# A transformer layer on one core: the first Strassen product ahead of the output projection, attention's QK one tile at a time, the softmax exp at the end of MLP2

## The chip, the core and the metric

The kernel runs on one core of a Trainium2 chip. The metric is the device time of one execution in microseconds (us), smaller is better. A timed run gives a time, the span of the core and the mean granted clock of TensorE over that span (1.0 is full speed). One execution is also taken by the hardware profiler; its page and its trace are quoted here. A run that is over 1.5% above the fastest of its kernel is counted as slow. Medians and ranges below are of all runs, ratios of the fast ones alone.

The engines in the profile are PE (TensorE's matmuls), PEld (its weight loads), DVE (VectorE), ACT (ScalarE), POOL (GpSimd) and SP (the queue that issues most DMAs). The kernel is scheduled by hand: each engine has its own list of instructions, so the order of two independent instructions on one engine is a decision. A hole is a stretch in which TensorE waits. The halo of a tile is the part of K or V that comes from earlier rows; a DMA fetches it. The gelu tail is what ScalarE still has to do of MLP1's gelus when TensorE has ended MLP1, about 2.8 us.

## The reference

A pre-norm layer on x of 2048 rows and 576 columns, bf16, one batch:

```python
def _A_ref(x, wqkv, wo):                 # H = 32 heads of 18, window W = 8, dilation 2
    qkv = ...(x @ wqkv)...
    idx = pos[:, None] - off[None, :]    # keys at distance 0, 2, .., 14
    logits = jnp.einsum("bhsd,bhswd->bhsw", q, kg) * scale
    attn = _softmax(jnp.where(mask, logits, -1e9))
    return einsum("bhsw,bhswd->bhsd", attn, vg)... @ wo
def _B_ref(x, w1, b1, w2, b2):           # F = 4608
    h = _gelu(_layernorm(x) @ w1 + b1)
    return h @ w2 + b2
h  = x + _A_ref(_layernorm(x), ...)
h2 = h + _B_ref(_layernorm(h), ...)
```

## The kernel before

The 16 token tiles of 128 rows go through the second half of the kernel in eight groups of two. While group k is in its MLP, the attention of group k+2 runs on VectorE (QK, softmax, PV), and group k+1 gets its output projection ("wo") and its second layer norm (LN2). So one turn of the loop contains, on TensorE: MLP1 of group k, the projection of k+1, MLP2 of k.

From group 2 on, MLP2 uses Strassen's scheme on a part of the hidden dimension: seven products instead of eight, on sums of blocks that VectorE prepares (`w2_sums`, `h_sums`); `rows` says how large that part is (8 of 18 pairs of blocks in groups 2 and 3, 12 in 4 and 5, all 18 in 6 and 7), the rest is done plainly. The products accumulate in PSUM banks a, b, d, f and e. Three times ScalarE copies a bank to another one, to be its starting value; this is called a seed here: b from a after product 1, d from b after product 6, f from d after product 5.

```python
def mlp2_fast(g, rows, tags, last, inserts):        # before; cut
    product(1, a, rows, True)
    seed(b, a)                       # ScalarE copy, PSUM to PSUM
    call(inserts.get(1, ()))         # ln2_stats(c, d), h_sums, w2_sums
    product(2, a, rows)              # has to wait until the seed has read bank a
    plain(0, 0, a, rows)
    call(inserts.get(2, ()))         # att_den(e, f)
    product(6, b, rows)
    seed(d, b)
    call(inserts.get(6, ()))         # ln2_send(c), ln2_send(d)
    product(7, e, rows, True)
    add(rest, e..., x_of(j1))
    call(inserts.get(7, ()))         # PV of tile e, ln2_ins
    product(5, d, rows)
    seed(f, d)
    product(4, b, rows); plain(1, 0, b, rows); plain(1, 1, d, rows)
    add(o1, bd, rest); store(j1, o1)
    call(inserts.get(4, ()))         # PV of tile f
    product(3, f, rows); plain(0, 1, f, rows)
    out0(...)
# the loop of one group, k >= 2; cut
    m1[1] = [c_(att_qk_pair, e, f)]  # QK of both tiles of group k+2, during MLP1
    mlp1(g, mlp1_plan(p, q, r, s, True), m1, mid)
    if e is not None:
        exps(e, f)                   # table load, exp, gelu's table load, on ScalarE
    if c is not None:
        wo_visit((c, q), (d, r))     # output projection of group k+1
    mlp2_fast(g, rows, (s, p, q), c is None, x)
```

LN2's statistics are on ScalarE too (`ln2_act`: two passes with accumulators, then a reciprocal root by a power instruction on GpSimd), and so is its application (`ln2_send`), which then goes out to DRAM and comes back through a transposing DMA (`ln2_in`) as the input of the next MLP1.

## Time and profile before

| | before |
|---|---|
| timed runs | 393.6 us median of 4 (392.1 to 394.3) |
| profiled run | 389.87 us, span 388.1 us, mean granted clock 0.995 |
| TensorE, VectorE, ScalarE busy | 361.8, 298.3, 229.8 us |
| TensorE waiting in MLP2 for ScalarE's seeds | 17.2 us in 12 waits |

The page of the kernel before, its first part (busy time, share, instructions) and the head of the fourth (the chain of waits that ended last):

```profile
PE 361.8 (93%) x4904; PEld 297.3 (77%) x4904; DVE 298.3 (77%) x412; ACT 229.8 (59%) x513; POOL 35.1 (9%) x47
...
PE 51%; DVE 32%; ACT 7%; issue 4%; DMA 2%; SPq 1%; POOL 1%; DVEq 0%; ACTq 0%; POOLq 0%
```

Up to about 152 us VectorE leads (LN1, the first tiles' attention). From there on it is TensorE and its holes. The view by windows, one line for each group 2 to 7 (start and end in us, length, then busy time and number of instructions of PE, PEld, DVE, ACT, POOL, then the granted clock, the DMA share and GB/s):

```profile
146.20:190.50 44.30, 38.96 (x498) 33.08 (x498) 35.76 (x40) 23.78 (x57) 2.89 (x4) 0.96 0.32 78
190.50:231.90 41.40, 37.10 (x499) 30.66 (x499) 31.72 (x37) 23.78 (x57) 2.88 (x4) 1.00 0.39 77
231.90:271.80 39.90, 36.62 (x495) 30.28 (x496) 35.21 (x40) 23.87 (x57) 1.95 (x4) 1.00 0.29 67
271.80:311.70 39.90, 36.62 (x495) 30.28 (x496) 33.02 (x37) 23.98 (x57) 2.65 (x5) 1.00 0.33 76
311.70:348.50 36.80, 35.80 (x489) 29.61 (x488) 18.42 (x31) 20.55 (x53) 2.61 (x4) 1.00 0.27 49
348.50:388.00 39.50, 33.77 (x451) 27.98 (x450) 8.90 (x13) 14.73 (x39) 0.00 (x0) 0.99 0.04 13
```

The first two numbers after the window are to be compared: group 2 lasts 44.30 us with 38.96 us of TensorE, group 4 lasts 39.90 us with 36.62 us. Where the difference is, TensorE's timeline shows. Each line has start, length, line, operation, operands and count, and in brackets how long the engine was idle before it and what ended that. Product 1 of group 2, the matmuls after the hole, and product 4:

```profile
167.44 1.16 PE L619 MATMUL po<-w2a_sb,h_all 128*128 128x288 bf16 x8
171.89 4.28 PE L619 MATMUL po<-w2a_sb,h_all 128*128 128x288 bf16 x20 [3.29 <-ACT po L650]
...
181.10 0.65 PE L619 MATMUL po<-x_all,h_all 128*128 128x288 f16 x4 [1.00 <-ACT po L650]
```

TensorE stands still for 3.29 us until the seed is copied. The 20 matmuls after it take 4.28 us; the same 20 in group 3 take 2.61 us. The window of that stretch shows why:

```profile
172.00:177.00 5.00, 5.00 (x29) 3.43 (x28) 2.98 (x5) 3.54 (x10) 1.11 (x2) 0.66 0.01 3
```

The granted clock is 0.66 over these 5 us. In group 3, after a hole of 3.30 us, it stays at 1.00.

What the seed waited for is in ScalarE's timeline, here of group 4, from the last gelus of MLP1 (which ends on TensorE at 249.7 us) to the seed:

```profile
248.04 4.49 ACT L528 ACTIVATE h_all<-pm,b_sb 128x256 f16<-128x256 f32 x12 [1.99 <-PE pm L214]
252.55 1.28 ACT L366 ACT_TABLE_LOAD   x1
253.84 0.63 ACT L366 ACTIVATE logits<-logits 128x512 f32<-128x512 f32 x1
254.49 1.28 ACT L504 ACT_TABLE_LOAD   x1
255.79 0.20 ACT L504 ACTIVATE warm<-mhalf 128x1 f32<-128x1 f32 x1
255.90 0.39 ACT L650 COPY po<-po 128x288 f32<-128x288 f32 x1
```

The gelus end at 252.5, then come a table load, the exp, the load of gelu's table and a dummy instruction that forces it, 3.4 us together, and only then the seed (L650).

### The profile page before, as it was taken

The page shows a single profiled execution, that of the slowest core. Times are in us where ns is not written, and L with a number is a line of the kernel's source. Part 1 is how long each engine was busy: PE and PEld are TensorE (multiplying, and loading weights), DVE is VectorE, ACT ScalarE, POOL GpSimd, SP SyncE. Part 2 cuts the span into 40 slices and gives each one's busy share as a digit, 9 for nine tenths or more (in the row PEclk, how much of TensorE's full clock was granted, in tenths as well). Part 3 has the DMA queues.
Part 4 walks back from the last instruction along what each step waited for, and adds up shares of the span by engine and source line. Part 5 has one row for each costly group of instructions (what it writes and reads, how often), then busy time and mean ns, then how long its engine had stood idle before and what let it go on. Part 6 is the DMA issues. An engine that isn't in the chain of part 4 may idle for free.

```text
span 388.1 us, 11433 instructions
## 1 busy us (share of the span) xinstructions
PE 361.8 (93%) x4904; PEld 297.3 (77%) x4904; DVE 298.3 (77%) x412; ACT 229.8 (59%) x513; POOL 35.1 (9%) x47
## 2 busy tenths in 40 slices
PE   7999999999999998968998799979997999999895
PEld 4789877896788777946886578857885788778774
DVE  6899999999998999895779579978977794420331
ACT  2687747887657833793087806781579247726710
POOL 3240021000220110000100110010101010100000
PEclk9999999999999999989999999999999999999999
DMA  8987798946296355201921074004710350040000
GB/s 244 309 247 221 167 236 265 350 67 188 68 196 183 138 101 112 64 30 51 157 70 47 20 153 106 17 30 111 149 19 31 94 107 17 3 84 17 2 9 24
DMA packets 61875, 43.70 MB, mean 113 GB/s; under 512 B 31856, under 2 KB 60144, under 8 KB 61824
## 3 DMA queue, kind: packets, MB, share of 16 engines
q1 hardware_dynamic: 59936, 41.13, 39.6%
q0 software_dynamic: 1728, 1.77, 4.4%
q8 instruction: 38, 0.62, 0.7%
q10 hardware_dynamic: 160, 0.07, 0.1%
q14 instruction: 13, 0.11, 0.1%
HBM read 21.10 MB, written 12.42 MB: 86 GB/s over the span
## 4 chain that ended last, share of the span: by engine, by line
PE 51%; DVE 32%; ACT 7%; issue 4%; DMA 2%; SPq 1%; POOL 1%; DVEq 0%; ACTq 0%; POOLq 0%
PE pm L214 25%; PE po L619 24%; DVE prod L381 5%; DVE prod L332 5%; DVE prod L326 5%; DVE prod L385 4%; ACT h_all L528 3%; DVE ln_stats L150 2%; PE pw L214 2%; DVE h L439 1%; DMA x_all<-in_A_x_dram 1%; ACT po L650 1%; ACT L504 1%; DVE peak L344 1%; PE pq L214 1%
## 5 line engine op out<-in xcount | busy, mean ns | idle before, releaser
L528 ACT ACTIVATE h_all<-pm,b_sb 128x256 f16<-128x256 f32 (+1 forms) x288 | 108.5, 498 | 94.4 <-PE pm L214 94.4
L214 PE MATMUL pm<-hnT,w_sb 64*128 64x256 bf16 x2304 | 143.1, 269 | 1.5 <-DVE o_sb L692 1.0
L214 PEld LDWEIGHTS <-w_sb 64*128 64x128 bf16 x2304 | 113.7, 94 | 15.1 <-issue 3.5
L619 PEld LDWEIGHTS <-h_all 128*128 128x128 f16 x560 | 55.1, 99 | 36.3 <-issue 22.2
L619 PE MATMUL po<-w2a_sb,h_all 128*128 128x288 bf16 (+1 forms) x332 | 47.3, 293 | 14.7 <-ACT po L650 13.3
L214 PE MATMUL pq<-wq_sb,xnT 64*128 64x288 bf16 x768 | 54.1, 283 | 0.3 <-ACT kv_ring L299 0.2
L214 PEld LDWEIGHTS <-xnT 64*128 64x128 bf16 x864 | 44.0, 94 | 9.1 <-issue 0.4
L332 DVE TENSOR_TENSOR prod<-prod 128x2304 bf16<-128x2304 bf16 (+1 forms) x64 | 44.2, 691 | 2.1
L326 DVE TENSOR_TENSOR prod<-kv_ring,q_all 128x4608 bf16<-128x4608 bf16 x16 | 40.8, 2549 | 6.4 <-DMA kv_ring<-kv_dram 6.3
L381 DVE TENSOR_TENSOR prod<-kv_ring,probs 128x4608 bf16<-128x4608 bf16 x16 | 40.8, 2552 | 0.2
L214 PE MATMUL pm<-hnT,w1h_sb 64*128 64x256 bf16 x288 | 39.5, 269 | 0.0
L385 DVE TENSOR_TENSOR prod<-prod 128x2304 bf16<-128x2304 bf16 (+1 forms) x32 | 33.8, 1058 | 1.1
L542 PEld LDWEIGHTS <-h_all 128*128 128x128 bf16 x288 | 28.0, 98 | 7.7 <-issue 0.7
L542 PE MATMUL po<-w2a_sb,h_all 128*128 128x288 bf16 x224 | 28.3, 286 | 0.0
L455 POOL TENSOR_TENSOR ln_rstd<-ln_var,mhalf 128x1 f32<-128x1 f32 x14 | 10.3, 733 | 198.2 <-ACT ln_var L454 196.8
L619 PEld LDWEIGHTS <-kv_ring 128*128 128x128 f16 x228 | 22.3, 98 | 5.6
L299 ACT CAST kv_ring<-pq 128x576 bf16<-128x576 f32 x32 | 19.4, 641 | 8.4 <-PE pq L214 8.2
L647 DVE TENSOR_TENSOR kv_ring<-po,x_all 128x576 f32<-128x576 f32 x6 | 4.5, 758 | 24.1 <-PE po L619 24.1
L599 DVE TENSOR_TENSOR kv_ring<-h_all 128x1536 f16<-128x1536 f16 (+2 forms) x8 | 6.3, 786 | 21.4 <-ACT h_all L528 21.4
L619 PE MATMUL po<-w2b_sb,h_all 128*128 128x288 bf16 (+1 forms) x152 | 22.2, 286 | 0.0
L214 PE MATMUL pw<-wo_sb,oT 64*128 64x288 bf16 x256 | 19.5, 283 | 0.2
L650 ACT COPY po<-po 128x288 f32<-128x288 f32 x18 | 6.9, 386 | 19.8 <-PE po L619 19.8
(97 smaller groups left out, 386.7 us busy)
## 6 DMA issues: line engine op xcount, KB each, us to landing
w_sb<-in_B_w_dram SPq DMA_DIRECT2D x6, 768.0 KB, 6.3
kv_ring<-kv_dram SPq DMA_DIRECT2D x28, 144.0 KB, 2.9
w2a_sb<-in_B_w_dram SPq DMA_DIRECT2D x4, 1008.0 KB, 6.4
kv_dram<-kv_ring SPq DMA_DIRECT2D x13, 288.0 KB, 4.7
out_dram<-o_sb SPq DMA_DIRECT2D x15, 144.0 KB, 2.0
td<-q_all SPq DMA_DIRECT2D x14, 144.0 KB, 2.2
td<-hn SPq DMA_DIRECT2D x14, 144.0 KB, 1.8
x_all<-in_A_x_dram SPq DMA_DIRECT2D x12, 144.0 KB, 2.3
```

The costliest lines, as they stand in the source:

```text
L150: nc.vector.bn_stats(out=stats[:, i, c, :], in_=src[:, c * HALF:(c + 1) * HALF])
L214: last = nc.tensor.matmul(duo["g"][r ^ swap][i], lhsT=lhsT, rhs=rhs, start=(swap == 0 and i == 0 and kt == 0), stop=(swap == 1 and kt == K ...
L299: pace[0] = nc.scalar.copy(out=dst.rearrange("p (d g h) -> p g d h", g=2, h=H // 2), in_=ps[:, :, 0:HALF].rearrange("p g (h d) -> p g d h" ...
L326: nc.vector.tensor_tensor(out=prod[:], in0=k_ring[j % 2], in1=q_all[:, j, :].unsqueeze(1) .to_broadcast([P, W, D]), op=ALU.mult)
L332: nc.vector.tensor_tensor(out=prod[:, :, o * H:o * H + n], in0=prod[:, :, a * H:a * H + n], in1=prod[:, :, c * H:c * H + n], op=ALU.add)
L381: nc.vector.tensor_tensor(out=prod[:].rearrange("p w (d h) -> p w d h", h=H), in0=v_ring[j % 2].rearrange("p w (d h) -> p w d h", h=H), in ...
L385: nc.vector.tensor_tensor(out=prod[:, 0:n, :], in0=prod[:, 0:n, :], in1=prod[:, n:2 * n, :], op=ALU.add)
L455: nc.gpsimd.tensor_tensor(out=rstd[:], in0=var[:], in1=mhalf[:], op=ALU.pow)
L528: pace[0] = nc.scalar.activation(out=hT(grp)[:, f, 0:N], in_=ps[:, r, i * N:(i + 1) * N], func=ACT.Gelu_apprx_tanh, bias=b1_sb[:, f:f + 1] ...
L542: nc.tensor.matmul(banks[half], lhsT=hT(grp)[:, f, i * P:(i + 1) * P], rhs=w2_rows(f)[:, half * HALF:(half + 1) * HALF], start=(f == 0), s ...
L619: nc.tensor.matmul(bank, lhsT=l, rhs=r, start=start, stop=stop, skip_group_check=True)
L650: nc.scalar.copy(out=to, in_=bank)
```

## The change

The intent is to fill the hole from both sides: product 1 goes ahead of the projection, so that its seed runs while TensorE does the projection, and exp with its two table loads goes behind the last seed of MLP2. Attention had to be taken apart for this, since normalization and PV follow exp: QK of tile e is now computed a turn earlier, in MLP2, and QK of tile f in MLP1, with the logits of alternate groups in two places; PV of tile e is at the end of MLP2 and PV of f at the start of the next MLP1. Half of `h_sums` moves into MLP1. The seeds get new places between the steps of LN2. The core of the diff, cut:

```diff
-        product(1, a, rows, True)
-        seed(b, a)
...
+        if rows <= SR:        # groups 2 to 5
+            steps = [(1, all_), "b", "wo", "h", "e", (2, all_), "11", (6, all_), "6", "d", "7", (7, all_), "rest", "in",
+                     (5, all_), "f", "exp", (4, all_), "21", "22", "o1", "4", (3, all_), "12", "o0", "3"]
+        elif not last:        # group 6
+            steps = [(1, lo), "wo", "h", "e", (1, hi), "b", (7, lo), (6, all_), "6", "d", "7", (2, all_), (7, hi), "rest", "in",
+                     (5, all_), "f", (4, all_), "o1", (3, all_), "o0"]
+        else:                 # group 7
+            steps = ["e", (1, lo), (7, lo), (1, hi), "b", "h", (7, hi), "rest", (6, all_), "d", (2, all_), "lo",
+                     (5, all_), "f", (4, all_), "o1", (3, all_), "o0"]
...
-                m1[1] = [c_(att_qk_pair, e, f)]
+                m1[0] += [c_(pv_sum, d), c_(send_o, d), c_(read_o, d)]
+                m1[1] = [c_(att_qk_one, f, 1, home ^ 1), c_(att_max, (e, f))]
+                m1[3] += [c_(h_sums, 0, rows, (0, 2))]
+                x["h"] += [c_(h_sums, 0, rows, (1, 3))]
+                x["exp"] += [c_(exps, e, f), c_(att_den, e, f)]
+                x["4"] += [c_(att_pv_a, e), c_(halo, e, 2)]
+                x["3"] += [c_(att_pv_b, e), c_(send_o, e), c_(read_o, e)]
...
+                x["7"] += [c_(att_qk_one, GROUPS[k + 3][0], 0, home)]
...
+                x["h"] = [c_(ln2_stats, c, d)] + x["h"]
+                x["6"] += [c_(ln2_send, c)]
+                x["7"] = [c_(ln2_send, d)] + x["7"]
+                x["in"] = [c_(ln2_ins, c, d)] + x["in"]
```

In `steps` a tuple is a product with its rows, a letter b, d or f is a seed, "wo" the projection, "11" to "22" the plain part, "o1" and "o0" the output sums; the others are hooks for the lists of `x`.

More of the change, by code (lines that the diff above doesn't have):

```diff
@@ L314, with logit_of @@
     side = {}
+    def logit_of(js):
+        home, i = side[js[0]]
+        return (x_all[:, 13:16:2, 0:2 * W * H].bitcast(F32).rearrange("p i (w h) -> p i w h", w=W)
+                if home else logits[:])[:, i:i + len(js)]
     def sides(js):
-        i = side[js[0]]
+        i = side[js[0]][1]
         return slice(i, i + len(js))
@@ L333, in att_qk_add, with att_qk_b @@
                                     in1=prod[:, :, c * H:c * H + n], op=ALU.add)
-    def att_qk_b(j, i, skip=0):
-        side[j] = i
+    def att_qk_b(j, i, skip=0, home=0):
+        side[j] = (home, i)
+        out = logit_of([j])[:, 0]
         att_qk_add(j, ((0, 0, 9), (0, 0, 4), (0, 0, 2), (0, 0, 1))[skip:])
-        nc.vector.tensor_tensor(out=logits[:, i], in0=prod[:, :, 0:H], in1=prod[:, :, 8 * H:9 * H], op=ALU.add)
+        nc.vector.tensor_tensor(out=out, in0=prod[:, :, 0:H], in1=prod[:, :, 8 * H:9 * H], op=ALU.add)
         if j // 2 + 1 < W:
-            nc.vector.memset(logits[0:1, i, j // 2 + 1:W, :], -1e9)
+            nc.vector.memset(out[0:1, j // 2 + 1:W, :], -1e9)
     def att_max(js):
-        n, sl = len(js), sides(js)
-        nc.vector.tensor_reduce(out=peak[:, sl], in_=logits[:, sl].rearrange("p i w h -> p i h w"), axis=AX.X, op=ALU.max)
-        nc.vector.tensor_tensor(out=logits[:, sl], in0=logits[:, sl],
-                                in1=peak[:, sl].unsqueeze(2).to_broadcast([P, n, W, H]), op=ALU.subtract)
+        n, sl, lg = len(js), sides(js), logit_of(js)
+        nc.vector.tensor_reduce(out=peak[:, sl], in_=lg.rearrange("p i w h -> p i h w"), axis=AX.X, op=ALU.max)
+        nc.vector.tensor_tensor(out=lg, in0=lg, in1=peak[:, sl].unsqueeze(2).to_broadcast([P, n, W, H]), op=ALU.subtract)
     def att_qk_rest(j, i, skip=0):
@@ L355, in att_qk, with att_qk_one @@
         att_qk_rest(j, i)
-    def att_qk_pair(e, f):
-        for i, j in enumerate((e, f)):
-            att_qk_a(j)
-            halo(j, 1)
-            att_qk_b(j, i)
-        att_max([e, f])
+    def att_qk_one(j, i, home):
+        att_qk_a(j)
+        halo(j, 1)
+        att_qk_b(j, i, 0, home)
     def att_exp(*js):
-        sl = sides(js)
-        nc.scalar.activation(out=logits[:, sl], in_=logits[:, sl], func=ACT.Exp, scale=SCALE)
+        lg = logit_of(js)
+        nc.scalar.activation(out=lg, in_=lg, func=ACT.Exp, scale=SCALE)
     def att_pv(j):
@@ L372, in att_den, with att_pv_a @@
     def att_den(*js):
-        n, sl = len(js), sides(js)
-        nc.vector.tensor_reduce(out=den[:, sl], in_=logits[:, sl].rearrange("p i w h -> p i h w"), axis=AX.X, op=ALU.add)
+        n, sl, lg = len(js), sides(js), logit_of(js)
+        nc.vector.tensor_reduce(out=den[:, sl], in_=lg.rearrange("p i w h -> p i h w"), axis=AX.X, op=ALU.add)
         nc.vector.reciprocal(out=den[:, sl], in_=den[:, sl])
-        nc.vector.tensor_tensor(out=probs[:, sl], in0=logits[:, sl],
-                                in1=den[:, sl].unsqueeze(2).to_broadcast([P, n, W, H]), op=ALU.mult)
-    def att_pv_sum(j):
-        a = probs[:, side.pop(j)]
+        nc.vector.tensor_tensor(out=probs[:, sl], in0=lg, in1=den[:, sl].unsqueeze(2).to_broadcast([P, n, W, H]), op=ALU.mult)
+    def att_pv_a(j):
+        a = probs[:, side.pop(j)[1]]
         nc.vector.tensor_tensor(out=prod[:].rearrange("p w (d h) -> p w d h", h=H),
@@ L383, in att_pv_sum, with att_pv_b @@
                                 in1=a.unsqueeze(2).to_broadcast([P, W, Dh, H]), op=ALU.mult)
+    def att_pv_b(j):
         for n in (4, 2):
@@ L386, in att_pv_sum @@
         nc.vector.tensor_tensor(out=q_all[:, j, :], in0=prod[:, 0, :], in1=prod[:, 1, :], op=ALU.add)
+    def att_pv_sum(j):
+        att_pv_a(j)
+        att_pv_b(j)
     oT, hn, hnT, h_of = {}, {}, {}, {}
@@ L619, in mm, with product @@
         nc.tensor.matmul(bank, lhsT=l, rhs=r, start=start, stop=stop, skip_group_check=True)
-    def product(n, bank, rows, start=False):
+    def product(n, bank, m0, m1):
         lhs, rhs = PRODUCTS[n]
-        for m in range(rows):
-            mm(bank, lhs(m), rhs(m), start and m == 0, m == rows - 1)
+        for m in range(m0, m1):
+            mm(bank, lhs(m), rhs(m), n in (1, 7) and m == 0, m == m1 - 1)
     def plain(i, half, bank, rows):
@@ L635, in halves, with mlp2_fast @@
         return ap.rearrange("p (g c) -> p g c", g=2)
-    def mlp2_fast(g, rows, tags, last, inserts):
+    def mlp2_fast(g, rows, tags, wo, hooks):
+        p, q, r, s = tags
+        last = wo is None
         j0, j1 = g
-        af, bd, ee = (psum_pair(tag, "po") for tag in tags)
+        af, bd = (psum_pair(tag, "po") for tag in (q, p))
         a, f, b, d = (pair[:, n, 0:HALF] for pair in (af, bd) for n in range(2))
-        e = ee[:, 0, 0:HALF]
         o0, o1 = (late.tile([P, D], BF16, tag="o_sb", name="o_sb", bufs=2) for _ in range(2))
@@ L644, in mlp2_fast @@
         rest = halves(flat[:, W * 2 * D - 2 * D:W * 2 * D].bitcast(F32))
+        bank = {1: a, 2: a, 3: f, 4: b, 5: d, 6: b}
         def add(out, x, y):
             nc.vector.tensor_tensor(out=out, in0=x, in1=y, op=ALU.add)
-        def seed(to, bank):
-            nc.scalar.copy(out=to, in_=bank)
-        def store(j, o, n=slice(0, 2)):
-            cols = slice(n.start * HALF, n.stop * HALF)
-            nc.sync.dma_start(out=out3[:, j, cols], in_=o[:, cols])
-        def out0(n=slice(0, 2)):
-            add(halves(o0[:])[:, n], af[:, n, 0:HALF], halves(x_of(j0))[:, n])
-            store(j0, o0, n)
@@ L660, in mlp2_fast @@
-        product(1, a, rows, True)
-        seed(b, a)
-        call(inserts.get(1, ()))
-        product(2, a, rows)
-        plain(0, 0, a, rows)
-        if last:
-            out0(slice(0, 1))
-        call(inserts.get(2, ()))
-        product(6, b, rows)
-        seed(d, b)
-        call(inserts.get(6, ()))
-        product(7, e, rows, True)
-        add(rest, e.unsqueeze(1).to_broadcast([P, 2, HALF]), halves(x_of(j1)))
-        call(inserts.get(7, ()))
-        product(5, d, rows)
-        seed(f, d)
@@ L676, in mlp2_fast, with out0 @@
-        call(inserts.get(5, ()))
-        product(4, b, rows)
-        plain(1, 0, b, rows)
-        plain(1, 1, d, rows)
-        add(halves(o1[:]), bd[:, :, 0:HALF], rest)
-        store(j1, o1)
-        call(inserts.get(4, ()))
-        product(3, f, rows)
-        plain(0, 1, f, rows)
-        out0(slice(1, 2) if last else slice(0, 2))
-        call(inserts.get(3, ()))
+        def out0(n0, n1):
+            add(halves(o0[:])[:, n0:n1], af[:, n0:n1, 0:HALF], halves(x_of(j0))[:, n0:n1])
+            nc.sync.dma_start(out=out3[:, j0, n0 * HALF:n1 * HALF], in_=o0[:, n0 * HALF:n1 * HALF])
@@ new lines, in out1, with do_rest, take_e @@
+        def out1():
+            add(halves(o1[:]), bd[:, :, 0:HALF], rest)
+            nc.sync.dma_start(out=out3[:, j1, :], in_=o1[:])
+        def do_rest():
+            add(rest, bank[7].unsqueeze(1).to_broadcast([P, 2, HALF]), halves(x_of(j1)))
+        def take_e():
+            bank[7] = psum_pair(r, "po")[:, 0, 0:HALF]
+        lo, hi, all_ = (0, min(rows, SR)), (SR, rows), (0, rows)
+        seed = {"b": (b, a), "d": (d, b), "f": (f, d)}
+        does = {
+            "wo": lambda: wo((r, s)), "e": take_e, "rest": do_rest, "o1": out1,
+            "o0": lambda: out0(int(last), 2), "lo": lambda: out0(0, 1),
+            "11": lambda: plain(0, 0, a, rows), "12": lambda: plain(0, 1, f, rows),
+            "21": lambda: plain(1, 0, b, rows), "22": lambda: plain(1, 1, d, rows),
+        }
@@ L688 @@
+        for step in steps:
+            if isinstance(step, tuple):
+                product(step[0], bank[step[0]], *step[1])
+            elif step in seed:
+                nc.scalar.copy(out=seed[step][0], in_=seed[step][1])
+            else:
+                call([does[step]] if step in does else hooks.get(step, ()))
     po_of = {}
@@ L789, in ln2_stats @@
                 (add_b2 if c == GROUPS[-1][0] else put_b2)(j)
-        def ln2_sends(c, d):
-            for j in (c, d):
-                ln2_send(j)
         def ln2_ins(c, d):
@@ L806, in ln2_pair @@
                 att_pv_sum(js[0])
-            ln2_sends(c, d)
+            ln2_send(c)
+            ln2_send(d)
             ln2_ins(c, d)
@@ L925 @@
                 ia[0] = [c_(wo_visit, (c, "B"), (d, "C")), c_(ln2_pair, c, d), c_(att_qk_b, f, 1, 2), c_(att_max, (e, f)),
-                         c_(exps, e, f)] + [c_(w2_sums, m, m + 4, (0, 1, 3)) for m in (0, 4)] + [c_(att_den, e, f)]
+                         c_(exps, e, f), c_(att_qk_one, GROUPS[4][0], 0, 1), c_(att_den, e, f)]
                 ia[2] = [c_(pv_sum, e), c_(dma_tr_o, e), c_(reload_x, GROUPS[4])]
                 ib[0] = [c_(finish_out, g[0])]
-                ib[2] = [c_(pv_sum, f), c_(dma_tr_o, f)]
-            elif e is not None:
-                m1[1] = [c_(att_qk_pair, e, f)]
             if k < 2:
@@ L937 @@
             rows = ROWS[k]
-            cuts = [m for m in (0, 12, 14, 16, NM) if m < rows] + [rows]
-            x = {n: [] for n in range(1, 8)}
-            if rows == NM:
+            home = k % 2
+            x = {n: [] for n in ("h", "6", "7", "in", "exp", "4", "3")}
+            if k < 6:
+                m1[0] += [c_(pv_sum, d), c_(send_o, d), c_(read_o, d)]
+                m1[1] = [c_(att_qk_one, f, 1, home ^ 1), c_(att_max, (e, f))]
+                m1[3] = []
+                if k == 2:
+                    m1[3] += [c_(w2_sums, m, m + 4) for m in (0, 4)]
+                if k == 3:
+                    m1[3] += [c_(w2_sums, 8, 12, (0, 1, 3))]
+                if k == 4:
+                    m1[3] += [c_(w2_sums, 8, 12, (2,))]
+                m1[3] += [c_(h_sums, 0, rows, (0, 2))]
[3 more added lines that the diff above has]
+                x["3"] += [c_(att_pv_b, e), c_(send_o, e), c_(read_o, e)]
+            else:
@@ L941 @@
                 if k == 6:
+                    m1[0] += [c_(pv_sum, d), c_(send_o, d), c_(read_o, d)]
                     m1[1] = [c_(w2_sums, *m) for m in ((12, 14), (14, 16), (16, NM))]
-                m1[3] = [c_(h_sums, 0, 12)]
-                x[1] = [c_(h_sums, 12, NM)]
-            else:
-                x[1] = [c_(h_sums, 0, rows, (0, 1))]
-                x[1] += [c_(w2_sums, m, m + 4, (2,)) for m in {2: (0, 4), 4: (8,)}.get(k, ())]
-                x[1] += [c_(h_sums, 0, rows, (2, 3))]
@@ L949 @@
-            if c is not None:
-                x[1] = [c_(ln2_stats, c, d)] + x[1]
-                x[6] += [c_(ln2_sends, c, d)]
-                x[7] += [c_(ln2_ins, c, d)]
-            if e is not None:
-                x[2] += [c_(att_den, e, f)]
-                x[7] = [c_(att_pv_sum, e), c_(halo, e, 2)] + x[7] + [c_(send_o, e)]
-                x[4] += [c_(pv_sum, f), c_(read_o, e), c_(send_o, f)]
-                x[3] += [c_(read_o, f)]
-            if k + 3 < len(GROUPS):
-                x[5] += [c_(reload_x, GROUPS[k + 3])]
@@ L960 @@
-            if k == 3:
-                x[3] += [c_(w2_sums, 8, 12, (0, 1, 3))]
-            mlp1(g, mlp1_plan(p, q, r, s, True), m1, mid)
-            if e is not None:
-                exps(e, f)
-            if c is not None:
-                wo_visit((c, q), (d, r))
-            mlp2_fast(g, rows, (s, p, q), c is None, x)
-            p, r = r, p
+                m1[3] = [c_(h_sums, 0, SR)]
+                x["h"] += [c_(h_sums, SR, NM, (0, 2)), c_(h_sums, SR, NM, (1, 3))]
+            if k + 3 < len(GROUPS):
+                x["7"] += [c_(att_qk_one, GROUPS[k + 3][0], 0, home)]
+                x["in"] += [c_(reload_x, GROUPS[k + 3])]
@@ L972 @@
+            wo = None
+            if c is not None:
+                x["h"] = [c_(ln2_stats, c, d)] + x["h"]
+                x["6"] += [c_(ln2_send, c)]
+                x["7"] = [c_(ln2_send, d)] + x["7"]
+                x["in"] = [c_(ln2_ins, c, d)] + x["in"]
+                wo = lambda tags: wo_visit((c, tags[0]), (d, tags[1]))
+            mlp1(g, mlp1_plan(p, q, r, s, True), m1, mid)
+            mlp2_fast(g, rows, (p, q, r, s), wo, x)
+            p, q, r, s = s, r, p, q
 _INS = ['A_x', 'A_wqkv', 'A_wo', 'B_x', 'B_w1', 'B_b1', 'B_w2', 'B_b2']
```

## The prediction

> **What bounds the kernel now.** In the chain of waits, TensorE holds 51% and VectorE 32%. VectorE's part lies mostly before 152 us; from there on (token groups 2 to 7) the kernel is TensorE work plus a few holes. The table by windows gives groups 2..7 as 44.3, 41.4, 39.9, 39.9, 36.8 and 39.5 us, with TensorE busy 39.0, 37.1, 36.6, 36.6, 35.8, 33.8. TensorE's timeline shows the holes of one group: after product 1 it waits for ScalarE's seed copy 3.29, 3.30, 2.81 and 2.8 us (groups 2 to 5), later 0.5 to 1.0 us for the seed before product 4; group 7 loses 1.38 + 0.53 + 0.47.
>
> Why: ScalarE's timeline at the end of MLP1 runs 2.85 us past TensorE with gelus, then table load 1.28, exp 0.63, table load 1.28, dummy 0.20, and only then the seed (0.39). [...] The output projection (2.2 us) runs before product 1 and hides only the gelus. In group 2 the hole is followed by 5 us at a granted clock of 0.66, about 1.7 us more.
>
> **The change.** No arithmetic is added or removed, nor a table load. Product 1 (1.0 to 1.5 us) goes ahead of the projection, so its seed runs under the projection; exp and both table loads go behind the last seed. VectorE does one QK (about 5.9 us) in MLP1 and one in MLP2, which also removes waits of 1.5 to 2.2 us for the halo of K, and half of the sums move into MLP1.
>
> **By group, from those durations.**
> - Group 1/2 border: the output sum no longer queues behind a PV (5.2 us) on VectorE: the 1.05 us hole at 151.4 us goes.
> - Groups 2 to 5: the first hole shrinks to 0.0 to 0.2. In groups 2 and 3 (eight product rows) the second seed now comes behind LN2's first send, so product 5 waits 0.3 to 1.8 us; the wait before product 4 stays at 0.5 to 0.7. In groups 4 and 5 the second seed is just in time. I get 40 to 41, 38, 36.8, 36.8 us: gains about 4 (with most of the clock dip), 3.3, 3.1, 3.1.
> - Group 6: **loss**. The seed is queued behind the LN2 statistics of both tiles (3.85 us on ScalarE), so product 6 waits about 2.5 us: 36.8 becomes 38 to 38.5.
> - Group 7: the rows of products 1 and 7 that are ready fill the gelu tail: gain about 1.9.
>
> Sum: 1 + 4 + 3.3 + 3.1 + 3.1 - 1.5 + 1.9 = about 14.9; I take off one for what I can't see. VectorE is the second limit: about 33 to 35 us of work in a group of 37 to 38. Groups 3 to 5 leave it 0.4 to 2 us before h is wanted.
>
> **Predicted: 379.5 us, range 375.5 to 385.5. Faster by over 2%: 0.89; within 2%: 0.10; slower: 0.01.**
>
> **In the profile after:** TensorE waiting for the seed copies in total falls from 17.2 us to about 8, most of it in group 6 and before product 4; no exp in the chain of waits; no hole over 3 us in MLP2; VectorE's waits for the K halo (6.3 us) nearly gone; VectorE over 85% busy in groups 2 to 5; the granted clock stays at 1.00 in group 2.
>
> **What would make it wrong:** VectorE late with h or with product 6's sums, so that one hole is exchanged for another; LN2's transposes landing after MLP2's end (before, about 1.2 us ahead; I expect 2 to 3); the V halo, now fetched between two PVs close together, delaying VectorE; the clock dipping elsewhere when TensorE is denser.

## The result, and the profile after

| | before | predicted | after |
|---|---|---|---|
| timed, median | 393.6 | 379.5 (375.5 to 385.5) | 380.8 (378.9 to 382.9), 4 runs |
| profiled run: span, clock | 388.1, 0.995 | | 379.3, 0.995 |
| start of group 2 | 146.2 | 146.2 | 146.6 |
| group 2 | 44.3 | 40 to 41 | 42.4 |
| group 3 | 41.4 | 38 | 39.0 |
| groups 4, 5 | 39.9, 39.9 | 36.8, 36.8 | 37.1, 37.1 |
| group 6 | 36.9 | 38 to 38.5 | 38.8 |
| group 7, to TensorE's last matmul | 36.1 | about 34.2 | 34.4 |

The lengths of groups are taken from the first MLP1 matmul of one group to that of the next, in TensorE's timeline. The ratio is 0.968 (95% interval 0.962 to 0.974). Ratios here are the mean time of one kernel's fast runs over that of the other's of the same rounds, so not quite the ratio of the medians quoted. The kernel is faster by 3.2%, and its time lies in the predicted range.

The page after, the same lines:

```profile
PE 362.6 (96%) x4904; PEld 295.0 (78%) x4904; DVE 299.1 (79%) x412; ACT 230.2 (61%) x513; POOL 43.7 (12%) x47
...
PE 70%; DVE 17%; ACT 6%; POOL 2%; issue 1%; DMA 1%; SPq 1%; POOLq 0%; DVEq 0%
```

TensorE's busy time has hardly changed (361.8 and 362.6 us), its share of the chain has grown from 51% to 70%, VectorE's has fallen from 32% to 17%. The view by windows after:

```profile
146.60:189.00 42.40, 38.82 (x499) 30.96 (x500) 36.69 (x45) 24.03 (x57) 5.84 (x4) 0.96 0.37 85
189.00:228.00 39.00, 37.26 (x497) 30.48 (x496) 34.10 (x39) 24.03 (x57) 5.84 (x4) 1.00 0.32 78
228.00:265.20 37.20, 36.73 (x495) 30.20 (x496) 33.43 (x37) 24.00 (x57) 3.70 (x4) 1.00 0.33 81
265.20:302.30 37.10, 36.63 (x494) 30.13 (x496) 27.31 (x30) 23.93 (x57) 3.05 (x5) 1.00 0.35 69
302.30:341.10 38.80, 36.05 (x489) 29.51 (x490) 23.46 (x35) 20.54 (x53) 1.43 (x3) 1.00 0.26 52
341.10:379.30 38.20, 33.69 (x451) 27.82 (x450) 8.93 (x13) 14.70 (x39) 0.00 (x0) 1.00 0.05 16
```

Groups 2 to 5 and 7 are shorter, group 6 is longer. TensorE's timeline after, the matmuls that waited: in group 2 products 5 and 4, in group 3 product 5:

```profile
176.59 0.65 PE L627 MATMUL po<-x_all,kv_ring 128*128 128x288 f16 x4 [3.00 <-ACT po L694]
...
178.24 1.12 PE L627 MATMUL po<-x_all,h_all 128*128 128x288 f16 x4 [0.47 <-ACT po L694]
```

```profile
216.99 0.65 PE L627 MATMUL po<-x_all,kv_ring 128*128 128x288 f16 x4 [1.27 <-ACT po L694]
```

And in group 6 product 6:

```profile
328.57 0.65 PE L627 MATMUL po<-x_all,kv_ring 128*128 128x288 f16 x4 [2.27 <-ACT po L694]
```

The hole before product 2 has gone in all four groups 2 to 5: no line there has a bracket any more. In groups 4 and 5 only the 0.47 us before product 4 are left. But group 2 has a new hole of 3.00 us before product 5, group 3 one of 1.27 us, and group 6 one of 2.27 us. In group 2 the clock dips here too:

```profile
177.00:182.00 5.00, 4.53 (x26) 2.95 (x25) 3.39 (x8) 4.45 (x6) 0.00 (x0) 0.66 0.50 131
```

The holes of groups 2 and 3 lead to GpSimd. Its timeline, the power instructions of LN2 (two of each group merged to one line where nothing lies between), before and after:

```profile
173.93 0.56 POOL L455 TENSOR_TENSOR ln_rstd<-ln_var,mhalf 128x1 f32<-128x1 f32 x1 [30.17 <-ACT ln_var L454]
175.82 0.55 POOL L455 TENSOR_TENSOR ln_rstd<-ln_var,mhalf 128x1 f32<-128x1 f32 x1 [1.33 <-ACT ln_var L454]
```

```profile
172.33 4.06 POOL L463 TENSOR_TENSOR ln_rstd<-ln_var,mhalf 128x1 f32<-128x1 f32 x2 [26.66 <-ACT ln_var L462]
...
212.73 2.69 POOL L463 TENSOR_TENSOR ln_rstd<-ln_var,mhalf 128x1 f32<-128x1 f32 x1 [27.12 <-ACT ln_var L462]
```

What took 0.56 and 0.55 us now takes 4.06 us for the two. VectorE's timeline shows what it did at that time:

```profile
172.04 2.55 DVE L331 TENSOR_TENSOR prod<-kv_ring,q_all 128x4608 bf16<-128x4608 bf16 x1
174.63 1.36 DVE L337 TENSOR_TENSOR prod<-prod 128x2304 bf16<-128x2304 bf16 x1
```

The QK multiply (L331) begins 0.29 us before the power instruction. The chain of waits has the first of the two powers alone (start, length, what):

```profile
172.33 2.70 POOL ln_rstd L463
175.05 0.30 ACT ln_nmean L468
```

It took 2.70 us, until 0.4 us after the end of the multiply, and only then does ScalarE go on (L468, part of `ln2_send(c)`). In ScalarE's program `ln2_send(c)` needs that power and stands ahead of the seed that product 5 needs. How long ScalarE waited for it, its timeline shows:

```profile
175.05 0.29 ACT L468 ACTIVATE ln_nmean<-ln_nmean,ln_rstd 128x1 f32<-128x1 f32 x1 [0.98 <-POOL ln_rstd L463]
```

It is 0.98 us, in group 3 too (at 215.45); the rest of the 2.70 us passes while ScalarE does the statistics of tile d. So the slow power makes 0.98 us of each of the two holes. The other 2.02 us in group 2 come from LN2 starting late: ScalarE had waited 2.57 us for VectorE's h (at 170.18), 0.55 us in group 3.

### The profile page after: what moved, and what is told of

Same layout as the page of the kernel before. It is cut to its first block, busy times and chain, and to the rows that moved or that the text cites. A ratio compares the mean times of both kernels' runs of the same rounds, so it can differ in the third digit from the quotient of the medians.

```text
span 379.3 us, 11422 instructions
## 1 busy us (share of the span) xinstructions
PE 362.6 (96%) x4904; PEld 295.0 (78%) x4904; DVE 299.1 (79%) x412; ACT 230.2 (61%) x513; POOL 43.7 (12%) x47
## 4 chain that ended last, share of the span: by engine, by line
PE 70%; DVE 17%; ACT 6%; POOL 2%; issue 1%; DMA 1%; SPq 1%; POOLq 0%; DVEq 0%
PE pm L214 31%; PE po L627 22%; PE po L550 9%; PE pw L214 4%; PE pq L214 3%; DVE prod L337 2%; DVE ln_stats L150 2%; DVE prod L383 2%; DVE prod L331 2%; ACT h_all L536 2%; DVE prod L389 2%; DMA x_all<-in_A_x_dram 1%; POOL ln_rstd L463 1%; ACT hn L461 1%; ACT po L694 1%
## 5 line engine op out<-in xcount | busy, mean ns | idle before, releaser
L627 PEld LDWEIGHTS <-h_all 128*128 128x128 f16 x560 | 54.3, 99 | 20.9 <-issue 6.4
L627 PE MATMUL po<-w2a_sb,h_all 128*128 128x288 bf16 (+1 forms) x332 | 46.5, 288 | 0.2 <-DVE h_all L607 0.2
L337 DVE TENSOR_TENSOR prod<-prod 128x2304 bf16<-128x2304 bf16 (+1 forms) x64 | 44.2, 691 | 2.1
L331 DVE TENSOR_TENSOR prod<-kv_ring,q_all 128x4608 bf16<-128x4608 bf16 x16 | 40.9, 2553 | 1.1 <-DMA kv_ring<-kv_dram 0.8
L463 POOL TENSOR_TENSOR ln_rstd<-ln_var,mhalf 128x1 f32<-128x1 f32 x14 | 19.0, 1357 | 189.1 <-ACT ln_var L462 189.1
L161 POOL TENSOR_TENSOR ln_rstd<-ln_veps,mhalf 128x1 f32<-128x1 f32 (+2 forms) x13 | 13.1, 1010 | 49.3 <-DVE ln_veps L155 41.9
L447 DVE TENSOR_TENSOR h<-pw,x_all 128x576 f32<-128x576 f32 x16 | 11.4, 750 | 8.4 <-PE pw L214 8.4
```

The costliest lines, as they stand in the source:

```text
L161: nc.gpsimd.tensor_tensor(out=rstd[:], in0=veps[:], in1=mhalf[:].to_broadcast([P, n]), op=ALU.pow)
L331: nc.vector.tensor_tensor(out=prod[:], in0=k_ring[j % 2], in1=q_all[:, j, :].unsqueeze(1) .to_broadcast([P, W, D]), op=ALU.mult)
L337: nc.vector.tensor_tensor(out=prod[:, :, o * H:o * H + n], in0=prod[:, :, a * H:a * H + n], in1=prod[:, :, c * H:c * H + n], op=ALU.add)
L447: nc.vector.tensor_tensor(out=h[:].rearrange("p (g c) -> p g c", g=2), in0=pw[:, :, 0:HALF], in1=x_of(j).rearrange("p (g c) -> p g c", g=2 ...
L463: nc.gpsimd.tensor_tensor(out=rstd[:], in0=var[:], in1=mhalf[:], op=ALU.pow)
L627: nc.tensor.matmul(bank, lhsT=l, rhs=r, start=start, stop=stop, skip_group_check=True)
```

## The experiments

Ten kernels were run in three lots; each lot has its own runs of the kernel before on the same chip. The timed results, and the group lengths of each profiled run:

| run | median us | ratio to before | groups 2, 3, 4, 5, 6, 7 |
|---|---|---|---|
| changed kernel | 380.8 | 0.968 | 42.4, 39.0, 37.1, 37.1, 38.8, 34.4 |
| e1 exp early | 391.0 | 0.998 | 42.5, 42.2, 39.9, 39.9, 38.8, 34.4 |
| e2 projection first | 380.1 | 0.968 | 42.0, 38.4, 37.6, 37.6, 38.8, 34.4 |
| e3 seed first in group 6 | 378.3 | 0.965 | 41.4, 39.0, 37.1, 37.1, 36.7, 34.4 |
| e4 before, with filler | 387.6 | 0.989 | 44.2, 41.4, 39.9, 39.9, 36.9, 36.1 |
| e5 QK later | 380.3 | 0.966 | 41.1, 37.9, 37.1, 37.1, 40.5, 34.4 |
| e6 seeds before sends | 378.1 | 0.960 | 39.8, 37.6, 37.1, 37.1, 40.5, 34.4 |
| e7 combined | 372.6 | 0.947 | 37.7, 37.4, 36.7, 36.7, 37.9, 34.4 |
| e8 extra VectorE work | 385.2 | 0.978 | 42.4, 41.0, 37.5, 37.3, 38.8, 34.4 |
| e9 combined, projection first in group 6 | 371.9 | 0.949 | 37.2, 37.4, 36.7, 36.7, 35.8, 34.4 |
| e7 again, with e9 | 372.5 | 0.951 | 37.2, 37.4, 36.7, 36.7, 37.5, 34.4 |

All outputs were correct. Two cautions for reading the table. The intervals of e2, e3, e5 and e6 overlap that of the changed kernel (0.962 to 0.974), so there the holes in the traces carry the reading, not the time. And one trace of group 2 is uncertain by about 1 us: e3 changes nothing before group 6, yet its group 2 is 1.0 us shorter than the changed kernel's (hole before product 5: 2.31 and 3.00 us). Group 3 is the same in both (39.0).

### e1: which part carries the gain, exp

```diff
-                x["exp"] += [c_(exps, e, f), c_(att_den, e, f)]
+                x["exp"] += [c_(att_den, e, f)]
...
+            if k < 6:
+                exps(e, f)
             mlp2_fast(g, rows, (p, q, r, s), wo, x)
```

> The changed kernel with exp and its two table loads put back to the end of MLP1, ahead of the first seed (product 1 still ahead of the output projection, QK still one tile at a time). Theory (the late exp is what removes the first hole): the seed ends 2.85 + 1.28 + 0.63 + 1.28 + 0.20 + 0.39 = 6.6 us after MLP1, product 2 could start at 3.2 (groups 2, 3) or 3.7 us (4, 5), so holes of about 3.4, 3.4, 2.9, 2.9 us come back before product 2; the holes before product 5 (3.0 and 1.3 us) go, as the seed is then late anyway. Net 8 us over the changed kernel: 387 to 392 us. Rival (the order of the products, or the QK spread over the pair, carries the gain): within 2 us of 380.8.

Measured: 391.0 us, ratio 0.998 (0.993 to 1.003), which is not told apart from the kernel before. The holes came back, of 3.19, 3.20, 2.71 and 2.70 us; two of them in TensorE's timeline:

```profile
170.97 4.12 PE L627 MATMUL po<-w2a_sb,h_all 128*128 128x288 bf16 x20 [3.19 <-ACT po L694]
```

```profile
255.68 2.12 PE L627 MATMUL po<-w2a_sb,h_all 128*128 128x288 bf16 x16 [2.71 <-ACT po L694]
```

With exp early, nearly all of the gain is gone, though product 1 is still ahead of the projection and QK still spread. (Group 3 is longer than in the kernel before because the clock dips after its hole, too (0.72 over 213.5 to 218.5 us); this trace has two dips and a mean clock of 0.990.)

### e2: which part carries the gain, the place of product 1

```diff
-            steps = [(1, all_), "b", "wo", "h", "e", (2, all_), "11", ...
+            steps = ["wo", (1, all_), "b", "h", "e", (2, all_), "11", ...
...
-            mlp2_fast(g, rows, (p, q, r, s), wo, x)
-            p, q, r, s = s, r, p, q
+            if k < 6:
+                mlp2_fast(g, rows, (p, s, q, r), wo, x)
+                p, r = r, p
+            else: ...
```

> The changed kernel with the output projection again ahead of product 1 in groups 2 to 5 (with the PSUM banks that the kernel before had for this), exp still late. Theory (the projection hid little that the gelu tail does not cost anyway): the seed can start at 3.5 to 4.0 us after MLP1 instead of 2.85, so a hole of about 0.65 us appears before product 2 in each of four groups, partly paid back because LN2 starts 1.0 to 1.5 us earlier (hole before product 5 in group 3 gone): 380 to 383.5 us, within 3 us of the changed kernel. Rival (product 1 ahead of the projection is the main part, as the change's title puts it first): 386 us or more.

Measured: 380.1 us, ratio 0.968, the same as the changed kernel. A hole of 0.53 us appears before product 2 in each of the four groups, about as expected (groups 4 and 5 are 0.5 us longer):

```profile
167.98 2.61 PE L627 MATMUL po<-w2a_sb,h_all 128*128 128x288 bf16 x20 [0.53 <-ACT po L694]
```

Group 3 is 0.67 us shorter, and its hole before product 5 is gone, since the projection and with it LN2 begin earlier; group 2 is 0.45 us shorter, which is within what one trace of it leaves uncertain. So what the title of the change puts first is, in groups 2 to 5, worth nothing that these runs can measure; it moves 0.5 us from one place to another.

### e3: the loss in group 6

```diff
-            steps = [(1, lo), "wo", "h", "e", (1, hi), "b", (7, lo), ...
+            steps = [(1, lo), "wo", (1, hi), "b", "h", "e", (7, lo), ...
```

> The changed kernel with one order changed in group 6: the seed of product 6 is issued on ScalarE ahead of LN2's statistics instead of behind them; TensorE's order is the same. Theory: the hole of 2.27 us before product 6 shrinks to 0.3 to 0.6 us (then VectorE's last sums, done 7.8 us after MLP1, release product 6's last rows); group 6 takes 36.9 to 37.3 us instead of 38.8, the whole about 379 us. Rival (the sums on VectorE, behind the adds of h and b2, are what product 6 waits for): the hole stays over 1.5 us and the time within 0.5 us.

Measured: 378.3 us (376.8 to 382.0), ratio 0.965. The trace has no hole before product 6 any more and group 6 lasts 36.7 us instead of 38.8, a little better than expected. The order on ScalarE was the cause of the loss, VectorE's sums were not.

### e4: the clock

```diff
         call(inserts.get(1, ()))
+        if rows < NM:
+            for _ in range(24 if rows == 8 else 20):
+                mm(e, h_block(0, 0, 0, 1), w2_block(0, 0, 0, 1), True, True)
         product(2, a, rows)
```

> The kernel before, with 24 (groups 2, 3) or 20 (groups 4, 5) useless matmuls into a free PSUM bank in the hole of about 3 us before product 2: more work, no wait taken away; the output is right. Its profiled run took 389.9 us but its timed runs 392.1 to 394.3, and its profile shows one dip of the granted clock (0.66 over 5 us) after one of the four holes. Theory A (holes of about 3 us sometimes drop the granted clock, about 1.7 us each time, and the timed runs had two or three such dips): 388.5 to 391 us, 2.5 to 5 us faster than the kernel before in the same rounds, mean granted clock 0.998 or more in every run. Theory B (dips don't matter beyond the one seen, the profiled run is an outlier for another reason): within 1.7 us of before, or slower.

Measured: 387.6 us against 392.4 in the same rounds, ratio 0.989 (0.986 to 0.992): 88 useless matmuls make the kernel before faster by 1.1% (the interval leaves out 1). The mean granted clock of its six runs was 0.998 to 1.000. That of the kernel before over 33 runs ran from 0.977 to 0.995, and the times follow it: 388.9 us in the one run at 0.995, 390.5 to 392.4 at 0.989 or 0.990, 392.3 to 393.6 at 0.985 or 0.986, 393.2 to 396.6 at 0.981, 394.4 to 396.2 at 0.977. TensorE's timeline of e4 has 0.35 us of hole left before product 2 in group 2 (before: 3.29):

```profile
173.52 2.61 PE L619 MATMUL po<-w2a_sb,h_all 128*128 128x288 bf16 x20 [0.35 <-ACT po L650]
```

The wait for the seed itself is as long as ever, since ScalarE's order is that of the kernel before. What the filler takes away is the dip of the clock after the hole (1.00 over groups 2 and 3 in its trace; 0.96 over group 2 before). The profiled run of the kernel before had one dip; its timed runs had, by their mean clock, about one to five (an estimate: one dip goes with 0.995 in this trace, two with 0.990 in that of e1). The profiled run of e4 (389.8 us) shows no gain, though it has no dip: group 2 lost 2.59 us at its start, waiting for VectorE's output sum, against 1.05 us before. It was the slowest of the six.

Why one hole of 3.3 us is followed by a dip and the next is not can be narrowed down from the traces. In the trace of the kernel before, the clock's record has its first entry 5.13 us after the kernel's first instruction, and the dip begins and ends 167.25 and 170.67 us after that entry; in the changed kernel's the first entry lies at 6.91 us, and the dip begins and ends 170.67 and 174.08 us after it. That is 49, 50, 50 and 51 steps of 3.413 us, to 0.02 us, and both dips last one such step at 0.50, which makes the 0.66 over 5 us: (5 - 3.413 / 2) / 5. The first line is the step before the dip of group 2 (kernel before), the second and third are the two steps over which the hole of group 3 is spread, the fourth is the one with the least work that no dip followed (group 4); then the changed kernel's step before its dip, and that of e5 in group 6 (window, length, then TensorE's busy time):

```profile
168.96:172.37 3.41, 0.48 (x4) 0.39 (x4) 3.38 (x6) 3.37 (x7) 0.00 (x0) 1.00 0.24 87
209.91:213.33 3.42, 1.74 (x20) 1.09 (x15) 3.12 (x5) 3.37 (x7) 0.00 (x0) 1.00 0.24 86
213.33:216.74 3.41, 1.79 (x15) 1.44 (x15) 2.96 (x5) 3.33 (x9) 0.00 (x0) 1.00 0.01 2
254.28:257.69 3.41, 1.35 (x12) 1.07 (x12) 3.41 (x5) 3.35 (x7) 0.00 (x0) 1.00 0.09 30
174.14:177.55 3.41, 0.96 (x8) 0.78 (x8) 3.24 (x6) 2.43 (x5) 2.25 (x2) 1.00 0.12 39
323.71:327.12 3.41, 1.13 (x10) 0.78 (x8) 2.83 (x6) 3.28 (x11) 1.25 (x2) 1.00 0.00 0
```

In the twelve traces all nine dips (leaving out the end of each kernel) follow a step in which TensorE was busy 0.12 (e8) to 0.33 (e5, e6) of the time, and no step with 0.40 or more (the 1.35 us of group 4 above) was followed by one. What lies between is not known, and what the hardware counts was not tested by a run of its own. But by these traces it is not the length of a hole alone that decides: holes of 3.29 us (before, group 2), 3.00 us (changed kernel, group 2) and 2.28 us (e5 and e6, group 6) were followed by a dip, holes of 3.30 us (before, group 3) and 2.27 us (changed kernel, group 6) were not. What differs is how the hole falls on the steps: the 2.27 us lie over two steps in which TensorE was busy 0.57 and 0.76, the 2.28 us of e5 in one with 0.33. And that differs from run to run.

### e5: GpSimd's power and VectorE's multiply

```diff
-                x["7"] += [c_(att_qk_one, GROUPS[k + 3][0], 0, home)]
-                x["in"] += [c_(reload_x, GROUPS[k + 3])]
+                qk = [c_(att_qk_one, GROUPS[k + 3][0], 0, home)]
+                x["7"] += qk if k == 4 else []
+                x["in"] += [c_(reload_x, GROUPS[k + 3])] + ([] if k == 4 else qk)
```

> The changed kernel with the QK that VectorE does in MLP2 moved behind the sum called rest in groups 2 and 3, so that VectorE runs no long bf16 multiply while GpSimd computes LN2's reciprocal root. Theory A (the power instruction of 0.56 us took 2.70 us because VectorE's 2.55 us multiply, begun 0.3 us before it[...]): the first power of groups 2 and 3 falls from 2.70 to 0.5 to 0.9 us, the hole before product 5 from 3.0 to about 1.5 us and from 1.27 to under 0.2; time 1 to 3 us under the changed kernel unless VectorE's lost 3 us come back as a late h in groups 3 and 4. Theory B (GpSimd is slow there for a reason of its own, for example the DMA issues in its queue): still over 2 us.

Measured: the powers take 0.55 to 0.56 us again in groups 2 and 3:

```profile
174.06 0.56 POOL L463 TENSOR_TENSOR ln_rstd<-ln_var,mhalf 128x1 f32<-128x1 f32 x1 [26.52 <-ACT ln_var L462]
175.95 0.55 POOL L463 TENSOR_TENSOR ln_rstd<-ln_var,mhalf 128x1 f32<-128x1 f32 x1 [1.33 <-ACT ln_var L462]
...
212.01 0.56 POOL L463 TENSOR_TENSOR ln_rstd<-ln_var,mhalf 128x1 f32<-128x1 f32 x1 [26.23 <-ACT ln_var L462]
```

The hole before product 5 fell from 1.27 to 0.18 us in group 3, and from 3.00 to 1.91 us in group 2, where VectorE was late with h and with product 6's sums in this run (a hole of 1.23 us before product 6). Groups 2 and 3 are shorter by 1.3 and 1.1 us; in group 3 that is the hole, but in group 2 the holes of MLP2 sum to more than before (3.61 us against 3.47), and what is gained there is the dip of the clock, which this run does not have in that group. The time, 380.3 us with a ratio of 0.966, does not show it beyond the noise: in the profiled run a dip of the clock (0.66 over 5 us, after the hole in group 6) made group 6 1.7 us longer. So theory A holds for the instruction; of the gain in time that was expected, nothing clear was seen. In these traces it goes by which of the two began first: at 175.95 the power began 0.09 us before the QK multiply (at 176.04) and took its usual 0.55 us, in the changed kernel it began 0.29 us after the multiply and took 2.70 us.

### e6: seeds before sends

```diff
-  (6, all_), "6", "d", "7", (7, all_), "rest", "in", (5, all_), "f", "exp", ...
+  (6, all_), "d", "6", "7", (7, all_), "rest", (5, all_), "f", "sd", "in", "exp", ...
...
-                x["7"] = [c_(ln2_send, d)] + x["7"]
+                x["sd" if k < 6 else "7"].insert(0, c_(ln2_send, d))
```

> The changed kernel with ScalarE's order changed in groups 2 to 5: the second seed ahead of LN2's first send, the third ahead of its second send (which moves behind it, with the transposing loads). Theory: the seed no longer waits for GpSimd's power, only for the statistics; hole before product 5 from 3.0 to about 1.1 us in group 2 and from 1.27 to 0 in group 3; the 0.47 us before product 4 stay; the dip of the clock in group 2 goes. 377 to 379 us. Rival (the wait only moves: the sends come late, the next MLP1 waits for the transposed input): a new hole at the start of groups 3 and 4, time within 1 us of the changed kernel.

Measured: 378.1 us, ratio 0.960 (0.956 to 0.965). The hole before product 5 is 0.83 us in group 2 and none in group 3, though the power is as slow as in the changed kernel (4.07 us for two). In group 2 a wait of 1.03 us before product 4 took the place of 0.47 us, because the third seed is still behind the first send. The sends are not too late: group 3 starts without a hole. Here, too, the profiled run dipped in group 6 (40.5 us; a clock of 0.66 over 324.4 to 329.4 us).

### e7: all repairs together

```diff
-  (2, all_), "11",  (6, all_), "6", "d", "7", (7, all_), "rest", "in", (5, all_), "f", "exp", ...
+  (2, all_), "11a", (6, all_), "d", "11b", "6", "7", (5, all_), "f", (7, all_), "rest", "sd", "in", "exp", ...
...  group 6:
+  [(1, lo), "wo", (1, hi), "b", "h", "e", (7, lo), (2, lo), (6, all_), "d", "6", "7", (2, hi),
+   (5, all_), "f", (7, hi), "rest", "in", (4, all_), "o1", (3, all_), "o0"]
...  group 2: h_sums (0, 1) and (2, 3) both after ln2_stats
```

> The changed kernel with all repairs: seed ahead of LN2's statistics in group 6; seeds ahead of the sends in groups 2 to 5; a third of the plain sums of product 2's bank kept as filler behind the second seed, product 7 moved behind the third seed as filler; in group 2 the first two sums of the product inputs behind h. Expected: no hole over 1 us in MLP2 of groups 2 to 6, group 2 about 39.5, group 3 about 37, groups 4 and 5 about 36.7, group 6 about 36 us, mean granted clock 0.998 or more; 372.5 to 376 us. If TensorE's holes are all filled but the time is over 377 us, the sum of holes is not what is left.

Measured: 372.6 us (371.0 to 377.0; 372.2 without the run that counts as slow), ratio 0.947 (0.943 to 0.950); it beats both kernels. In groups 2 to 6 TensorE waits once, 0.26 us before product 6 in group 2. Each seed now has independent matmuls behind it; even the 0.47 us before product 4 are covered, by product 7. Four of its six runs had a granted clock of 1.000, and the one at 0.995 was the slowest (377.0 us). But group 7 starts late, on LN2's transposing load:

```profile
334.06 0.61 PE L214 MATMUL pm<-hnT,w_sb 64*128 64x256 bf16 x8 [2.06 <-DMA hnT<-td]
```

### e8: room on VectorE

```diff
+                def extra():
+                    nc.vector.tensor_tensor(out=prod[:, 0:4, :], in0=prod[:, 0:4, :], in1=prod[:, 4:8, :], op=ALU.add)
+                m1[3] += [extra, extra] if k > 2 else []
                 m1[3] += [c_(h_sums, 0, rows, (0, 2))]
```

> The changed kernel with two useless bf16 adds of 1.37 us each on VectorE at the end of MLP1 in groups 3 to 5 (2.75 us a group; the output stays right). Theory (VectorE is the second limit: in the changed kernel it waits 0.6 us before h in group 3 and 2.1 us in group 4): h is late by about 2.1 us in group 3 and 0.7 us in groups 4 and 5, and the hole before product 5 grows by about as much, time 3 to 5 us over the changed kernel. Rival (80% busy leaves room for 2.75 us anywhere): within 1 us of it.

Measured: 385.2 us, ratio 0.978 (0.972 to 0.984) against 0.968. In the trace group 3 is 2.0 us longer (the hole before product 5 grew from 1.27 to 3.00 us), groups 4 and 5 are 0.4 and 0.2 us longer, together 2.6 us for 8.25 us of added work. The timed difference is 4.4 us by the medians; two of the four runs had a clock of 0.986 and 0.990. VectorE was busy 87% of group 3 and 90% of group 4 in the changed kernel and yet had about 2 us of room in group 4 (2.75 us of added work cost 0.4).

### e9: the wait that e7 uncovered

```diff
   group 6:
-  [(1, lo), "wo", (1, hi), "b", "h", "e", (7, lo), ...
+  ["wo", (1, all_), "hc", "b", "h", "e", (7, lo), ...      # "hc": h and statistics of c, "h": those of d
```

> The combined kernel with group 6 alone changed once more: the output projection ahead of product 1, ScalarE's seed between LN2's statistics of the two tiles. In the combined kernel TensorE has no hole in group 6, but group 7 then starts 2.06 us late, on the transposed LN2 output. Theory (with the holes filled, LN2's chain of about 16 us from the end of the projection bounds group 6, so starting the projection 1.5 to 2.2 us earlier starts group 7 earlier): the wait for the transposing load at the start of group 7 falls from 2.06 to under 0.5 us, no hole over 0.3 us before product 2; 1.2 to 2 us under the combined kernel on the same chip. Rival (the transposing loads are slow because of other DMA traffic at that time, 5.1 us to landing instead of 2.7): the wait stays over 1.5 us.

> The combined kernel again, unchanged, on the same chip as the run before, to compare the two: 372 to 374 us, again a wait of about 2 us for the transposing load at the start of group 7.

Measured: e9 371.9 us (371.2 to 373.1), e7 again 372.5 us (371.8 to 375.9), on one chip. The wait at the start of group 7 was 0.20 us in e9 and 1.66 us in e7:

```profile
331.18 0.61 PE L214 MATMUL pm<-hnT,w_sb 64*128 64x256 bf16 x8 [0.20 <-DMA hnT<-td]
```

```profile
332.24 0.61 PE L214 MATMUL pm<-hnT,w_sb 64*128 64x256 bf16 x8 [1.66 <-DMA hnT<-td]
```

Group 6 is 1.7 us shorter in the trace, but the medians differ by 0.5 us only and the times of the two overlap, so e9 is not shown to be faster. The transposing loads landed 3.8 us after issue in e9 and 4.3 us in e7, against 2.7 us in the changed kernel; why they are slower there was not found, so the rival is partly right.

## Why the prediction was right, and where it was not

**Right**: 379.5 predicted, 380.8 measured. But the two are so close partly because two errors cancel, and this is the most useful thing to learn here.

**The mechanism of the first hole was right.** The hole before product 2 is gone in four groups. e1 shows that exp and its table loads are what made it: with them back, the span is 388.1 us again and the time that of the kernel before. The prediction named both moves together as the cause; e2 shows that the place of product 1 contributes nothing measurable in groups 2 to 5. Moving it was only the way to hide the gelu tail of 2.85 us, and the projection ahead of product 1 (2.2 us) hid most of that already. What the spreading of QK is worth by itself was not run; e1 shows only that it brings no gain while exp is early.

**Groups 4 and 5 were right to 0.3 us** (36.8 against 37.1), **group 7 to 0.2 us**, and **the loss in group 6 was right in sign, cause and about in size**: 38 to 38.5 predicted, 38.8 measured; e3 took it back with one move on ScalarE.

**Groups 2 and 3 were mis-sized.** The step was "product 5 waits 0.3 to 1.8 us"; it waited 3.00 and 1.27 us. The missing term was GpSimd's power, costed at the 0.56 us of the trace before. It took 2.70 us, since the QK multiply that the change moves into MLP2 runs on VectorE at that moment, and held ScalarE up for 0.98 us. Without that the holes would be about 2.0 and 0.3 us (an estimate: 3.00 - 0.98 and 1.27 - 0.98), near the two ends of what was said; e5 measured 1.91 and 0.18. What the traces show of it: the power took 0.56 us with VectorE idle (before, group 3, at 216.98; e5, group 2, at 174.06), beside a reciprocal begun at 173.77 (before, group 2, at 173.93) and beside a tensor_reduce begun at 132.13 (before, at 132.15), and 2.70 and 2.69 us when the 2.55 us multiply had begun 0.29 us first (changed kernel, groups 2 and 3). The added time lies inside the power's own busy time, and the profile shows no wait for it. Why the power is slower beside the multiply was not shown. The lesson is that a duration in the trace of before is that of before's neighbours. That trace had a warning: in an earlier stage, under the multiply of a PV (97.12 to 99.67), a power took 1.66 us:

```profile
98.42 1.66 POOL L455 TENSOR_TENSOR ln_rstd<-ln_var,mhalf 128x1 f32<-128x1 f32 x1 [34.99 <-ACT ln_var L454]
```

**The dip of the clock in group 2 was predicted to go, and stayed**: 0.66 over 5 us again, after the new hole of 3.00 us. Group 2 gained 1.9 us instead of the 5 of the sum (4, and 1 for the border). Its holes account for that: 1.05 at the border, 3.29 before product 2 and 0.53 of the 1.00 before product 4 are gone, 3.00 before product 5 are new (1.87 us), and the dip, put at 1.7 us, is in both traces.

**What was left out altogether is the clock in the timed runs.** The prediction subtracted about 14 us, counted in a profiled run, from a timed level of about 393.4 (379.5 + 13.9; it does not name the number). In the traces, which both have a clock of 0.995, the change gives only 388.1 - 379.3 = 8.8 us. The timed gain is 12.8 us by the medians. The profiled run of before was one of its quickest; its timed runs had a mean clock of 0.986 over the 33 runs of the experiments, those of the changed kernel 0.999, 0.995, 0.994 and 0.985. About 4 us of the gain (12.8 - 8.8, an estimate; the mean clocks, 0.993 and 0.986 over some 390 us, give about 3) go with the higher clock, that is with fewer dips after TensorE's holes. That dips cost the kernel before more than that, about 4.8 us by the medians, e4 shows. The hint was on the page: a profiled time of 389.87 against timed runs of 392.1 and more.

**Of the signs to look for**: TensorE's waits for seeds fell from 17.2 to 9.4 us (about 8 predicted); no exp is left in the chain of waits after the start of group 2; VectorE's wait for the K halo fell from 6.3 to 0.8 us; there was no hole over 3.0 us, but one of exactly that; VectorE was over 85% busy in groups 2 to 4 (86.5, 87 and 90%), but not in group 5 (74%), which has no next QK to do, and that was to be seen in the diff.

**What was said could go wrong**: LN2's transposes were in time in the changed kernel; they became a limit only in e7, when TensorE's part of group 6 was short enough. VectorE's room was near what was said: e8's 2.75 us a group cost 2.0 us in group 3 and 0.2 to 0.4 in groups 4 and 5.

## What to carry to other kernels

ScalarE worked through its list in order here, and a long side job (exp with two table loads, 3.4 us, or the statistics of two tiles, 3.8 us) became a wait of TensorE, which needed the short copy (0.39 us) behind it: 3.29 us before product 2, 2.27 us before product 6. So put the short copy that releases the bottleneck engine ahead, and put matmuls that depend on nothing behind it. When an instruction is moved, look at what it will run beside (the power took 2.70 us instead of 0.56), not only at what it depends on. And compare the profiled run with the timed runs before subtracting from either: a difference of 1% was here a clock that some executions lost after a hole, and then a hole cost more than it lasted (1.67 us more: 4.28 against 2.61 us for the same 20 matmuls).
